# Moving a softmax scale from GpSimd to VectorE, with 1/sum in the PSUM tile of the chunk transposed first, the last output block spread around f tiles 14 and 15, and a rearranged start

## The chip, the cores and the metric

The kernel runs on one core of one Trainium2 chip. The metric is the device time in microseconds (us), lower is better. Every run quoted below is fast unless the text says otherwise; the mean granted TensorE clock was 0.993 to 0.999 of full speed in the profiled runs.

## The reference, cut to what matters

```python
# x (8, 4096, 192), weight_gen (8, 4096, 8 heads, 7 taps)
w = exp(weight_gen - max);  w = w / (sum(w over the 7 taps) + 1e-9)
conv[b, s, h, g] = sum over k of w[b, s, h, k] * x_padded[b, s + k, h, g]     # a causal convolution with its own weights per token
h = conv.reshape(32768, 192) @ w_in        # (192, 2048)
g = h - tanh(h)
out = g @ w_out                            # (2048, 192), float32
```

There are 32 token blocks of 1,024 tokens. For each block a softmax over the taps, seven products (one for each tap), their sum together with a transposition, a first matmul layer with 16 f tiles of 128 columns, `h - tanh(h)`, and a second layer with eight output blocks.

## The kernel before

The work is spread over five engines: ScalarE takes exp, tanh and the copies out of PSUM; VectorE takes the softmax sums, their reciprocals and the subtraction; GpSimd multiplies the softmax (`scale`) and the seven products; TensorE adds the products up in PSUM by multiplying with the identity (the "transposes", three 64-column chunks a block) and does both layers. Blocks are pipelined: while TensorE runs the first layer of block n it also runs the second layer of block n-1, the transposes of block n+1, and GpSimd forms the products of block n+2 with the softmax of n+3 made ready.

These parts are touched. `psum_h` is a pool of three PSUM tiles with one tag, given out in turn to the transposes (`pc`) and to the f tiles of the first layer (`ph`). Whoever asks for a tile gets the one that was used longest ago, and must wait until its last reader is done.

```python
psum_h = tc.tile_pool(name="psum_h", bufs=3, space=PSUM)
...
def softmax_norm(n, bank=None):
    e_t = e_of.pop(n)
    nc.vector.reduce_sum(out=zsum[:], in_=e_t...)
    if bank is None:                                   # every block but the first two
        nc.vector.reciprocal(zr[:], zsum[:])           # 1/sum in SBUF
        wsm_of[n] = (wsm, None, e_t, zr)               # GpSimd will scale: wsm = e_t * zr
        return
    ...
def products(n, ...):
    if e_t is not None:
        first = scale(nc.gpsimd, wsm[:], e_t, zr[:])
    ...                                                # then seven products on GpSimd
def gemm1(n, f):                                       # one f tile of the first layer
    ph = psum_h.tile(..., tag="ph")
    ... 6 matmuls into ph ...                           # "x12" in a timeline is two f tiles
    th = tanh(ph) on ScalarE;  gt = ph - th on VectorE # this subtraction frees ph
...
for n in range(NTOT):
    if n + 3 < NTOT:
        load_wg(n + 3)
        load_x(n + 3)                                  # at the top of the block
    for p in range(J):
        gemm1(n, 2 * p)
        gemm1(n, 2 * p + 1)
        ...
        if 1 <= n < NTOT - 1 and p == 6:               # after f tiles 12 and 13
            sums = conv_sums(n + 1, ((0, 1),), pcs)    # chunks 0 and 1 first
            gemm2((n - 1) * J + 6, between=...)        # mixed with an output block
            conv_out(n + 1, ((0, 1),), pcs)
            conv(n + 1, (2,))                          # then chunk 2
            gemm2((n - 1) * J + 7, 0, FILL)            # 4 matmuls of the last output block
        if p == 6 and n + 3 < NTOT:
            softmax_norm(n + 3)
        if 1 <= n < NTOT - 1 and p == 7:               # after f tiles 14 and 15
            gemm2((n - 1) * J + 7, FILL, NFT)          # its other 28
```

The softmax here doesn't subtract the row's maximum and nothing guards it: scores larger than these inputs give would overflow.

Of the kernel before, what the change touches and what calls it, by code (L numbers as in the profile page):

```python
# [16 lines left out]
def kernel(  # L17
# [8 lines left out]
    nc = tc.nc  # L26
# [52 lines left out]
    last_wsm = {}  # L79
# [19 lines left out]
    def load_x(n):  # L99
# [5 lines left out]
        def rows(p0, p1, r0=0, r1=HALO + J):  # L105
            win = x[b, s0 + p0 * J - HALO + r0 : s0 + p0 * J - HALO + r0 + 1]
            nc.sync.dma_start(  # L107
                out=x_t[p0:p1, r0:r1, :],
                in_=bass.AP(
                    tensor=win.tensor,  # L110
                    offset=win.offset,
                    ap=[[J * D, p1 - p0], [D, r1 - r0], [1, D]],
                ),
            )
# [8 lines left out]
        if n == 0:  # L123
            rows(0, P, HALO, HALO + J)
            rows(16, P, 0, HALO)
            rows(1, 16, 0, HALO)
            no_halo()
        elif s == 0:
            no_halo()
            rows(0, 1, HALO, HALO + J)  # L130
            rows(1, 16)
            rows(16, P)
        else:
            rows(0, P)
        x_of[n] = x_t

    def softmax_exp(n):
        wg_t = wg_of.pop(n)
        e_t = wgpool.tile([P, J, H, K], FP32, name="e_t")
        nc.scalar.activation(  # L140
# [6 lines left out]
    def softmax_norm(n, bank=None):  # L147
# [4 lines left out]
        )  # L152
        wsm = wgpool.tile([P, J, H, K], FP32, name="wsm")
        if bank is None:
            zr = wgpool.tile([P, J * H], FP32, name="zr")
            nc.vector.reciprocal(zr[:], zsum[:])  # L156
            wsm_of[n] = (wsm, None, e_t, zr)
            return

        zr = bank[:, 512 - J * H : 512]  # L160
        nc.vector.reciprocal(zr, zsum[:])
        wsm_v = bank[:, 0 : J * H * K].rearrange("p (j h k) -> p j h k", j=J, h=H)
        scale(nc.vector, wsm_v, e_t, zr)
        last_wsm[0] = scale(nc.vector, wsm[:], e_t, zr)
        wsm_of[n] = (wsm, wsm_v, None, None)
# [8 lines left out]
    def products(n, on_vector=(), order_of=None, sums=None, hooks={}, behind=None):  # L174
        x_t = x_of.pop(n)
        wsm, wsm_v, e_t, zr = wsm_of.pop(n)
        if e_t is not None:
            first = scale(nc.gpsimd, wsm[:], e_t, zr[:])
            if behind is not None:


                order(first, behind, "pace")
# [12 lines left out]
        for k in order_of or range(K):  # L195
            eng, w = (nc.vector, wsm_v) if k in on_vector else (nc.gpsimd, wsm[:])
            eng.tensor_mul(  # L197
                dst[k].rearrange("p c j h g -> p j h c g"),
                x_t[:, k : k + J, :].rearrange("p j (h c g) -> p j h c g", h=H, c=NC),
                w[:, :, :, k : k + 1]  # L200
                .rearrange("p j h (k o) -> p j h k o", o=1)
                .to_broadcast([P, J, H, NC, GC]),
            )
            if k == K - 2 and in_pairs:
# [17 lines left out]
    def conv_sums(n, parts, pcs):  # L222
# [5 lines left out]
        pcs.extend(psum_h.tile([P, 2, HT], FP32, name="pc", tag="ph") for _ in parts)  # L228
        if parts[-1][-1] == NC - 1:
            prods_of.pop(n)  # L230

        for gi in range(max(len(g) for g in prods)):
            for chunks, pc in zip(parts, pcs):
                some = [c for c in chunks if gi < len(prods[c])]
                last = gi == max(len(prods[c]) for c in chunks) - 1
                for c in some:
                    for j in range(JH):
                        col = ((c - chunks[0]) * JH + j) * R
                        for r in range(2):
                            nc.tensor.matmul(  # L240
                                pc[:, r, col : col + R],
# [9 lines left out]
    def conv_out(n, parts, pcs):  # L251
        for chunks, pc in zip(parts, pcs):
            c0, nch = chunks[0], len(chunks)
            nc.scalar.activation(  # L254
                out=conv_of[n][:, c0 : c0 + nch, :].rearrange(
                    "p c (j r t) -> p r (c j) t", r=2, t=R
                ),
                in_=pc[:, :, 0 : nch * JH * R].rearrange("p r (cj t) -> p r cj t", t=R),
                func=ACT.Copy,
            )  # L260
# [28 lines left out]
    LEAD, MIX, FILL = 6, 5, 2  # L289
# [82 lines left out]
    def load_w_in(f0, f1):  # L372

        for c in range(NC):
            src = moe_w_in[c * GC : c * GC + 1, f0:f1]
            dma = nc.gpsimd.dma_start(
                out=w_in[0:R, c, f0:f1],
                in_=bass.AP(
                    tensor=src.tensor,
                    offset=src.offset,  # L380
                    ap=[[G * F, H], [F, GC], [1, f1 - f0]],
                ),
            )
            if f0 == 0:

                order(dma, last_wsm[0], "order of the loads")

    def copy_w_in(f0, f1, eng):
        eng.dma_start(out=w_in[R:P, :, f0:f1], in_=w_in[0:R, :, f0:f1])

    def rest_of_w_in():
        load_w_in(FA, F)

    load_wg(0)
    load_x(0)
    softmax_exp(0)
    softmax_norm(0, obank[0])
    load_wg(1)
    load_x(1)
    load_w_in(0, FA)  # L400
    products(
        0,
        on_vector=(6, 3, 4, 5),
        order_of=(6, 0, 3, 1, 4, 5, 2),
        sums=(6, 3, 0, 4, 5, 1, 2),
        hooks={2: rest_of_w_in},
    )
    softmax_exp(1)
    softmax_norm(1, obank[1])
    load_wg(2)  # L410
    copy_w_in(0, FA, nc.scalar)
    copy_w_in(FA, F, nc.sync)
    products(1, on_vector=(0, 1), hooks={4: load_w_out})
    conv(0, (0, 1), (2,))
    load_x(2)
    for n in range(NTOT):
# [3 lines left out]
        for p in range(J):  # L420
            gemm1(n, 2 * p)
            gemm1(n, 2 * p + 1)
            if n == 0 and p == 1:
                softmax_exp(2)
            if p == 5 and n + 3 < NTOT:
                softmax_exp(n + 3)
            if n >= 1 and (p < 6 or n == NTOT - 1):
                gemm2((n - 1) * J + p)
            if p == 0 and 1 <= n < NTOT - 2:
                products(n + 2, behind=last_sub[0] if n > 1 else None)  # L430
            if n == 0 and p == 7:
                conv(1, (0, 1))
                conv(1, (2,))
# [54 lines left out]
```

## Time and profile before

| | before |
|---|---|
| time, median of 4 runs | 768.37 us |
| a quiet token block, from transposes to transposes | 22.56 us |
| TensorE / GpSimd / VectorE / ScalarE busy in it | 22.56 / 22.18 / 19.93 / 19.77 us |
| second block's first first-layer matmul | 43.05 us |
| one hole of TensorE near 64 us | 3.17 us, and a granted clock of 0.50 for 3.41 us after it |

The block row is the windows view of the kernel before, one quiet block. Its columns are the stretch, its length, then the busy time and number of instructions of TensorE, its weight loads, VectorE, ScalarE and GpSimd, the granted clock, the mean busy share of the DMA engines and GB/s.

```profile
591.44:614.00 22.56, 22.56 (x468) 17.83 (x462) 19.93 (x19) 19.77 (x29) 22.18 (x10) 1.00 0.63 156
```

TensorE is busy for all of it, GpSimd for all but 0.38 us. The other lines of this profile are in the prediction, with what they mean. "issue" in the chain of waits is time in which the engine waits for nothing that the profile shows; `[0.26 <-X]` after an instruction is the idle time before it and what ended it.

### The profile page before, as it was taken

The page shows a single profiled execution, that of the slowest core. Times are in us where ns is not written, and L with a number is a line of the kernel's source. Part 1 is how long each engine was busy: PE and PEld are TensorE (multiplying, and loading weights), DVE is VectorE, ACT ScalarE, POOL GpSimd, SP SyncE. Part 2 cuts the span into 40 slices and gives each one's busy share as a digit, 9 for nine tenths or more (in the row PEclk, how much of TensorE's full clock was granted, in tenths as well). Part 3 has the DMA queues.
Part 4 walks back from the last instruction along what each step waited for, and adds up shares of the span by engine and source line. Part 5 has one row for each costly group of instructions (what it writes and reads, how often), then busy time and mean ns, then how long its engine had stood idle before and what let it go on. Part 6 is the DMA issues. An engine that isn't in the chain of part 4 may idle for free.

```text
span 767.6 us, 32329 instructions
## 1 busy us (share of the span) xinstructions
PE 737.2 (96%) x14784; PEld 577.8 (75%) x14784; DVE 652.8 (85%) x595; ACT 637.1 (83%) x865; POOL 695.3 (91%) x290
## 2 busy tenths in 40 slices
PE   2798999999999999999999999999999999999997
PEld 2276787777777777777777777777778777777777
DVE  7886898888888888889888889888888988888883
ACT  1876888888888888888888888888888888888883
POOL 6999999999999999999999999999999999999100
PEclk9999999999999999999999999999999999999999
DMA  7913776555677555577655567755556765542412
GB/s 216 202 56 87 182 181 161 119 138 150 164 182 176 135 129 145 149 178 183 166 125 129 150 160 182 180 126 139 144 149 175 182 174 114 129 141 77 98 44 84
DMA packets 25989, 111.37 MB, mean 145 GB/s; under 512 B 4815, under 2 KB 9855, under 8 KB 21893
## 3 DMA queue, kind: packets, MB, share of 16 engines
q1 hardware_dynamic: 14830, 77.00, 30.2%
q0 software_dynamic: 10816, 31.99, 25.8%
q8 instruction: 115, 1.88, 1.0%
q10 hardware_dynamic: 208, 0.34, 0.2%
q14 instruction: 20, 0.16, 0.1%
HBM read 54.49 MB, written 25.17 MB: 104 GB/s over the span
## 4 chain that ended last, share of the span: by engine, by line
PE 93%; DVE 3%; POOL 1%; issue 1%; DMA 1%; ACT 0%; SPq 0%; POOLq 0%
PE obank L306 43%; PE ph L273 43%; PE pc L240 6%; DVE gt L285 2%; PE po L341 1%; DMA x_t<-zero 1%; POOL even L197 1%; ACT th L284 0%; POOL odd L197 0%; SPq L107 0%; DVE zr L156 0%; DVE zsum L150 0%; ACT convT L254 0%; SPq L93 0%; DVE out_sb L353 0%
## 5 line engine op out<-in xcount | busy, mean ns | idle before, releaser
L285 DVE TENSOR_TENSOR gt<-ph,th 128x1024 bf16<-128x1024 f32 x512 | 602.7, 1220 | 94.6 <-ACT th L284 92.1
L284 ACT ACTIVATE th<-ph 128x1024 f32<-128x1024 f32 x512 | 497.4, 1022 | 65.9 <-PE ph L273 65.2
L306 PE MATMUL obank<-w_out,gt 64*128 64x192 bf16 x7936 | 399.2, 243 | 1.4 <-issue 0.6
L306 PEld LDWEIGHTS <-gt 64*128 64x128 bf16 x7936 | 351.4, 94 | 52.6 <-issue 1.2
L273 PE MATMUL ph<-convT,w_in 64*128 64x512 bf16 x3072 | 384.8, 378 | 6.3 <-DVE gt L285 5.1
L197 POOL TENSOR_TENSOR even<-x_t,wsm 128x1536 bf16<-128x1536 f32 x94 | 273.0, 2904 | 3.1 <-DMA x_t<-zero 0.7
L197 POOL TENSOR_TENSOR odd<-x_t,wsm 128x1536 bf16<-128x1536 f32 x93 | 270.0, 2904 | 0.0
L273 PEld LDWEIGHTS <-w_in 64*128 64x128 bf16 x3072 | 176.4, 94 | 112.1 <-issue 18.8
L325 ACT ACTIVATE out_sb<-obank 128x192 f32<-128x192 f32 x248 | 82.4, 332 | 30.6 <-PE obank L306 23.5
L197 POOL TENSOR_TENSOR last<-x_t,wsm 128x1536 bf16<-128x1536 f32 x31 | 103.4, 3335 | 0.0
L240 PE MATMUL pc<-ident,even 64*128 64x64 bf16 x2304 | 70.3, 191 | 3.7 <-POOL even L197 2.4
L240 PEld LDWEIGHTS <-even 64*128 64x128 bf16 x2304 | 64.7, 96 | 5.0 <-POOL even L197 2.7
L254 ACT ACTIVATE convT<-pc 128x1024 bf16<-128x1024 f32 x64 | 48.8, 808 | 14.9 <-PE pc L240 14.8
L206 POOL DMA_DIRECT2D even<-odd x29 | 34.9, 1205 | 9.1 <-POOL odd L197 9.1
L168 POOL TENSOR_TENSOR wsm<-e_t,zr 128x448 f32<-128x448 f32 x30 | 41.7, 1391 | 0.0
L240 PE MATMUL pc<-ident,last 64*128 64x64 bf16 x768 | 23.2, 192 | 8.5 <-DVE last L197 8.3
L140 ACT ACTIVATE e_t<-wg_t 128x448 f32<-128x448 f32 x32 | 18.5, 577 | 7.0 <-DMA wg_t<-in_weight_gen_dram 7.0
L240 PEld LDWEIGHTS <-last 64*128 64x128 bf16 x768 | 17.0, 96 | 8.7 <-DVE last L197 8.3
L240 PE MATMUL pc<-ident,odd 64*128 64x64 bf16 x448 | 16.2, 199 | 6.7 <-issue 3.9
L150 DVE TENSOR_REDUCE zsum<-e_t 128x64 f32<-128x448 f32 x32 | 19.5, 609 | 3.0 <-ACT e_t L140 3.0
L156 DVE RECIPROCAL zr<-zsum 128x64 f32<-128x64 f32 x30 | 16.6, 554 | 3.0
L240 PEld LDWEIGHTS <-odd 64*128 64x128 bf16 x448 | 11.8, 100 | 7.4 <-issue 4.2
(20 smaller groups left out, 48.7 us busy)
## 6 DMA issues: line engine op xcount, KB each, us to landing
x_t<-in_x_dram SPq DMA_DIRECT2D x24, 1344.0 KB
even<-odd POOLq DMA_DIRECT2D x29, 1024.0 KB, 8.8
out_dram<-out_sb SPq DMA_DIRECT2D x31, 768.0 KB
x_t<-in_x_dram SPq DMA_DIRECT2D x7, 1176.0 KB
wg_t<-in_weight_gen_dram SPq DMA_DIRECT2D x32, 224.0 KB
x_t<-in_x_dram SPq DMA_DIRECT2D x7, 157.5 KB
x_t<-in_x_dram SPq DMA_DIRECT2D x1, 768.0 KB
w_out<-in_moe_w_out_dram POOLq DMA_DIRECT2D x1, 768.0 KB, 9.1
```

The costliest lines, as they stand in the source:

```text
L140: nc.scalar.activation(out=e_t[:].rearrange("p j h k -> p (j h k)"), in_=wg_t[:].rearrange("p j h k -> p (j h k)"), func=ACT.Exp,)
L150: nc.vector.reduce_sum(out=zsum[:], in_=e_t[:].rearrange("p j h k -> p (j h) k"), axis=AX.X)
L168: return eng.tensor_mul(wsm.rearrange("p j h k -> p (j h) k"), e_t[:].rearrange("p j h k -> p (j h) k"), zr.rearrange("p (n o) -> p n o", ...
L197: eng.tensor_mul(dst[k].rearrange("p c j h g -> p j h c g"), x_t[:, k : k + J, :].rearrange("p j (h c g) -> p j h c g", h=H, c=NC), w[:, : ...
L206: nc.gpsimd.dma_start(out=even[:].rearrange("p i c j h g -> p (i c j h g)")[:, 0:ACC], in_=odd[:].rearrange("p i c j h g -> p (i c j h g)" ...
L240: nc.tensor.matmul(pc[:, r, col : col + R], lhsT=prods[c][gi][r * R : (r + 1) * R, c, 2 * j : 2 * j + 2].rearrange("p j h g -> p (j h g)") ...
L254: nc.scalar.activation(out=conv_of[n][:, c0 : c0 + nch, :].rearrange("p c (j r t) -> p r (c j) t", r=2, t=R), in_=pc[:, :, 0 : nch * JH * ...
L273: nc.tensor.matmul(ph[:, r, :], lhsT=w_in[r * R : (r + 1) * R, c, f * P : (f + 1) * P], rhs=convT[r * R : (r + 1) * R, c, :], start=(c == ...
L284: last_act[0] = nc.scalar.activation(out=th[:], in_=ph_f, func=ACT.Tanh)
L285: last_sub[0] = nc.vector.tensor_sub(gt[:], ph_f, th[:])
L306: mm = nc.tensor.matmul(po[:, 0:D], lhsT=g_of[n][f][r * R : (r + 1) * R, col : col + P], rhs=w_out[r * R : (r + 1) * R, f, :], start=(r == ...
L325: last_act[0] = nc.scalar.activation(out=out_sb[:, j, :], in_=po[:, 0:D], func=ACT.Copy)
```

## The change

The intent: take the scale (1.39 us a block) off GpSimd, the engine that has no free time, and give it to VectorE in a form that was not to disturb GpSimd, with 1/sum in a PSUM tile; let the start overlap better, so that the second block begins earlier. A PSUM tile for 1/sum is at hand just then: that of the chunk transposed first, which ScalarE has just copied out. The chunk order is turned, (2) ahead of (0, 1), and the last output block is spread in three pieces around f tiles 14 and 15.

```diff
 def softmax_norm(n, bank=None, for_gpsimd=True, for_vector=False):
...
+        zr_v = bank[:, 512 - J * H : 512]
+        nc.vector.reciprocal(zr_v, zsum[:])          # 1/sum into the PSUM tile
+        if for_gpsimd:
+            scale(nc.vector, wsm[:], e_t, zr_v)      # VectorE scales
...
 # the end of a block
-                sums = conv_sums(n + 1, ((0, 1),), pcs)
...
+        sums = conv_sums(n + 1, ((2,),), pcs)
+        gemm2((n - 1) * J + 6, between=...)
+        conv_out(n + 1, ((2,),), pcs)
+        conv(n + 1, (0, 1))
+        gemm2((n - 1) * J + 7, 0, FILL)              # FILL = 2:  4 matmuls
+        if n + 3 < NTOT:
+            softmax_norm(n + 3, pcs[0][:, 0])
+        gemm1(n, NFT - 2)                            # f tile 14
+        gemm2((n - 1) * J + 7, FILL, HALF)           # HALF = 9: 14 matmuls
+        gemm1(n, NFT - 1)                            # f tile 15
+        gemm2((n - 1) * J + 7, HALF, NFT)            # 14 matmuls
...
 # the start: x of block 1 held behind block 0's first halo product; w_in's load issued
 # behind the first exp and half of its copy done by ScalarE; the taps of block 0 in pieces on
 # VectorE; softmax of block 2 ahead of the loop, of block 3 in block 1; transposes of
 # block 1 in the gaps of block 0, in the two output banks
+                if p == 3:
+                    sums = conv_sums(1, ((0, 1),), pcs, obank)
+                if 3 <= p <= 6:
+                    some(sums, (3 if p == 3 else 1) * 4 * JH)
```

Three small things go with it: the load of x at the start of a sequence is one transfer instead of three, the order that paces GpSimd by a subtraction of VectorE is put on its first product instead of on its scale, and `LEAD, MIX` (where and how densely transposes are mixed into an output block) are 5, 4 instead of 6, 5.

## The prediction

> **What bounds the kernel now.** I read the busy row and the chain of waits of the page first, then the waits of TensorE, then one undisturbed token block closely, then the start-up.
>
> ```profile
> PE 737.2 (96%) x14784; PEld 577.8 (75%) x14784; DVE 652.8 (85%) x595; ACT 637.1 (83%) x865; POOL 695.3 (91%) x290
> ...
> PE 93%; DVE 3%; POOL 1%; issue 1%; DMA 1%; ACT 0%; SPq 0%; POOLq 0%
> ```
>
> TensorE is busy 96% of the span and carries 93% of the chain that ended last. GpSimd at 91% is close, but its part of the chain is 1%, and in the list of TensorE's waits it occurs only in the start-up (2.4 us in two waits). So relieving GpSimd buys nothing by itself in the middle of the run. The interval from one convT copy to the next is 22.54 to 22.57 us in the quiet blocks; over 28 blocks (91.60 to 727.17) it averages 22.70.
>
> The timeline of one quiet block, TensorE and then VectorE, where the first chunk products are transposed and f tiles 14 and 15 follow:
>
> ```profile
> 610.23 1.48 PE L273 MATMUL ph<-convT,w_in 64*128 64x512 bf16 x12
> ...
> 614.56 1.47 PE L273 MATMUL ph<-convT,w_in 64*128 64x512 bf16 x12
> 615.85 1.34 PE L306 MATMUL obank<-w_out,gt 64*128 64x192 bf16 x28
> 617.01 1.57 PE L273 MATMUL ph<-convT,w_in 64*128 64x512 bf16 x12
> ```
>
> ```profile
> 612.15 2.36 DVE L285 TENSOR_TENSOR gt<-ph,th 128x1024 bf16<-128x1024 f32 x2 [0.26 <-ACT th L284]
> 614.43 0.61 DVE L150 TENSOR_REDUCE zsum<-e_t 128x64 f32<-128x448 f32 x1
> 615.14 0.55 DVE L156 RECIPROCAL zr<-zsum 128x64 f32<-128x64 f32 x1
> 616.48 4.81 DVE L285 TENSOR_TENSOR gt<-ph,th 128x1024 bf16<-128x1024 f32 x4 [0.79 <-ACT th L284]
> ```
>
> The reader is to see that f tile 14 starts at 614.56, while VectorE is still busy with the subtractions of tiles 12 and 13 until 614.5 and then with the sums and their reciprocal until 615.69; after that it has 0.79 us free. In the chain, twelve first-layer matmuls take 1.29 us; the pair at 614.56 takes 1.32 and the one at 617.01 takes 1.39. So the present order costs 0.13 us a block, a small wait for a PSUM buffer that a subtraction frees.
>
> The start-up: VectorE works without a pause through the first block (16 subtractions at 1.13 us, two softmax sums and reciprocals), and the second block's first matmul starts at 43.05. Then there is one real hole:
>
> ```profile
> 63.95 1.02 ACT L254 ACTIVATE convT<-pc 128x1024 bf16<-128x1024 f32 x1 [0.66 <-PE pc L240]
> 68.45 0.60 ACT L254 ACTIVATE convT<-pc 128x512 bf16<-128x512 f32 x1 [3.48 <-PE pc L240]
> ```
>
> ```profile
> 64.29 3.17 issue
> 67.46 0.95 PE pc L240 x29
> 68.41 0.32 PE obank L306 x4
> 68.73 2.44 PE ph L273 x12
> ```
>
> TensorE stands for 3.17 us in the midst of 168 transposes, with nothing recorded that it waits for, and then runs at a granted clock of 0.50 from 68 to 70. With the slow matmuls (2.44 for 1.29, 0.95 for about 0.43, some more) I put the hole at 4.9 us.
>
> [...] the transposes are the densest instruction stretch (15 ns per matmul with its weight load), and the x load of 1.3 MB keeps the DMA share near 1 from 61 to 64. The trace does not name the cause. [...] the scale then reads e_t from SBUF and 1/sum from PSUM. In the start-up that form took 0.62 to 0.63 us beside GpSimd at its usual pace. [...]
>
> **The change part by part, steady blocks.**
>
> Removed: GpSimd's scale, 1.39 us a block, from an engine whose 22.2 us of 22.56 does not set the end: 0. The 0.13 us of buffer wait goes too, because tiles 14 and 15 and the next tile 0 are now 14 second-layer matmuls apart.
>
> Unchanged: the counts of TensorE's work (104 transposes, 96 first-layer and 256 second-layer matmuls a block).
>
> Added: a 0.62 us scale on VectorE, before the subtraction of tile 14. Its 0.79 us of free time nearly holds it, so VectorE's own sequence is hardly pushed. But the PSUM tile of the first-transposed chunk is now released by that scale. There are three such tiles in rotation: tile 12 in X, 13 in Y, the first chunk in Z, the second in X, tile 14 in Y, tile 15 in Z. So tile 15's matmuls wait for the scale.
> - Tile 14 starts at 614.56 as before (the same work lies ahead of it). Six matmuls are 0.65, and 14 second-layer matmuls at 41 ns (1.32/32) are 0.58: tile 15 is ready at 615.79.
> - VectorE: the reciprocal ends at 615.69, 0.04 to the next instruction, 0.62 for the scale: 616.35; with about 0.06 for the signal (as from the subtraction of tile 14 to the matmul it frees at present) TensorE goes on at 616.41. A wait of 0.62 us.
> - From there: 0.65, 0.58 for 14 matmuls, and 1.29 for the next block's tiles 0 and 1: 618.93. Before: 617.01 + 1.39 = 618.40. Net +0.53 a block.
> - Later waits: subtraction 14 would end at 617.5, 15 near 619.3, 0' near 620.6; their buffers are wanted by TensorE at 618.3, 620.3 and 620.9. All in time, so nothing is added and nothing won back.
>
> It occurs in the 28 blocks that still normalise a later one: +14.8. The two others win 0.13 each: -0.3.
>
> **The start-up.** The w_in load is issued at about 4 instead of 6.9, and x of block 1 is held back, so x of block 0 arrives alone (1.8 MB with the weights of the softmax at some 350 GB/s from 2.1: about 7.3 instead of 9.4). GpSimd takes the tap that needs no halo from about 6.2 and then two more at 2.87 us pitch: 14.9 instead of 18.16. With the 1.78 us from there to the first first-layer matmul at present (18.16 to 19.94) that starts at 16.7 instead of 19.94. VectorE: its taps in pieces end near 13.5, the softmax of block 1 near 15.7, two taps of block 1 near 19.1, the softmax of block 2 near 20.3; so its first subtraction starts at 20.3 (before: 22.49), and no softmax lies among the 16 subtractions any more, which end at 38.5 instead of 43.0. The transposes of block 1 go into the two output banks in the gaps that VectorE leaves TensorE. The last tap of block 1 on GpSimd comes at about 33 (before 35.35), early enough. ScalarE's two copies and the third chunk put the second block's first matmul at 38.6 instead of 43.05: -4.5. The softmax of block 3 moves into block 1: 1.15 us on VectorE, of which 0.26 fits in its gap, so about +0.8.
>
> The hole at 64: the same burst of transposes meets the same x load, some 3 to 4 us earlier. But the instruction boundaries, the mix (4 instead of 5) and the load's form shift. I give it one half to vanish: -2.4.
>
> Sum: 768.3 - 4.5 + 0.8 + 14.8 - 0.3 - 2.4 = 776.7, so 776.5.
>
> **The rivals.**
> 1. GpSimd was the hidden bound, and VectorE's scale is hidden. For it: GpSimd has no idle time between blocks, 22.2 busy of 22.56. Against it: the accumulate DMA issued at 618.59 lands in 8.8 us, 7 us and more before its transposes. Then steady blocks gain only the 0.13: 768.3 - 3.7 - 3.9 = about 761, and 756 without the hole.
> 2. The wait is larger: the reciprocal is held by ScalarE's copy, or subtraction 14 is pushed and a second buffer is late. ScalarE's copy of the first chunk should end near 614.4, before the reciprocal, which speaks against it. With 0.3 us more a block: 785.
> 3. The start-up gains less, because the w_in pieces or x of block 1 come late (x of block 1 is only issued after 9.6 and must land by 15.7) or VectorE still has work ahead. Then -1.5 instead of -4.5: 780; with the hole as before, 782.
>
> **Range and chances.** The wait at tile 15 rests on durations that repeat in every block, so I hold it for likely (some 70%): 773 to 782 by the hole and the start-up. Rival 1 has some 20%, and rivals 2 and 3 fill the upper end. Range 762 to 783. Faster by over 2% means below 752.9, which needs everything to go right at once: 0.04. Slower by over 2% means above 783.6: 0.11. Within 2%: 0.85.
>
> **What would show each step.** In the waits of TensorE a new row of first-layer matmuls waiting for VectorE's scale, some 28 times and 0.6 us each; steady blocks of about 23.1 instead of 22.56; GpSimd's busy share down by some 39 us in the whole, with idle time; 1.39 turned into 1.29 at tiles 0 and 1. In the start-up the first subtraction near 20.3 and the second block's first matmul near 38.6. If the blocks stay at 22.4 to 22.6, the wait at tile 15 is wrong, and the time is near 760. The hole is seen as an "issue" piece of over 2 us with a clock of 0.50 after it, or its absence.

Its 350 GB/s are an estimate; in the windows view of before the DMA engines moved 334 GB/s from 2.1 to 9.0 us, at a share of 1.02, which would give 7.5 instead of 7.3. The 0.62 to 0.63 us are the scales at 15.73 and 16.40 in before, beside a product of GpSimd that took 2.90.

## The result, and the profile after

| | before | after |
|---|---|---|
| median of 4 runs | 768.37 us | 781.08 us |
| lowest to highest | 768.07 to 769.78 | 780.94 to 781.58 |
| quiet block | 22.56 us | 23.28 us |
| second block's first first-layer matmul | 43.05 us | 38.31 us |

The ratio of after to before is 1.0163, with a 95% interval of 1.0145 to 1.018: slower, by less than 2%. Ratios here are the mean time of one kernel's fast runs over that of the other's of the same rounds, so they are not quite the ratio of the medians quoted. The predicted 776.5 was 4.6 us low, inside the predicted range.

The busy row and the chain of the page after:

```profile
PE 738.7 (95%) x14784; PEld 576.7 (74%) x14784; DVE 672.4 (86%) x625; ACT 642.0 (82%) x869; POOL 670.1 (86%) x263
...
PE 86%; ACT 4%; issue 4%; DVE 4%; DMA 1%; ACTq 0%; SPq 0%; DVEq 0%
```

GpSimd is relieved (91% to 86%), VectorE hardly more loaded, TensorE does the same matmuls. But TensorE's part of the chain falls from 93% to 86%; ScalarE enters it with 4%, VectorE goes from 3% to 4% and "issue" from 1% to 4%. That is the mark of a wait that has come into every block.

One quiet block after, TensorE in the timeline, from the last second-layer matmuls before f tile 14 on (columns: start, length, engine, line, operation, output and inputs, shapes, number):

```profile
623.74 0.82 PE L290 MATMUL ph<-convT,w_in 64*128 64x512 bf16 x6
624.38 0.76 PE L324 MATMUL obank<-w_out,gt 64*128 64x192 bf16 x14
625.77 0.82 PE L290 MATMUL ph<-convT,w_in 64*128 64x512 bf16 x6 [0.64 <-ACT th L301]
626.42 0.76 PE L324 MATMUL obank<-w_out,gt 64*128 64x192 bf16 x14
627.00 1.48 PE L290 MATMUL ph<-convT,w_in 64*128 64x512 bf16 x12
```

VectorE and ScalarE in the same timeline:

```profile
623.60 0.61 DVE L152 TENSOR_REDUCE zsum<-e_t 128x64 f32<-128x448 f32 x1
624.34 0.56 DVE L162 RECIPROCAL pc<-zsum 128x64 f32<-128x64 f32 x1
625.00 0.62 DVE L175 TENSOR_TENSOR wsm<-e_t,pc 128x448 f32<-128x448 f32 x1
625.72 1.22 DVE L302 TENSOR_TENSOR gt<-ph,th 128x1024 bf16<-128x1024 f32 x1
```

```profile
623.05 1.73 ACT L273 ACTIVATE convT<-pc 128x512 bf16<-128x512 f32 x2
624.67 1.02 ACT L301 ACTIVATE th<-ph 128x1024 f32<-128x1024 f32 x1
```

Tile 15's first matmul (625.77) has 0.64 us of idle time in front of it. Its PSUM tile is the one that holds 1/sum, and VectorE's scale reads it from 625.00 to 625.62. The profile names another releaser, ScalarE's tanh of tile 14 (624.67 + 1.02 = 625.69), which ended a little later. The same in the waits of the kernel after (columns: us in total, times, longest):

```profile
PE ph L290 <- ACT th L301: 15.9, 25, 0.6
...
PE ph L290 <- DVE wsm L175: 0.5, 1, 0.5
```

26 waits of 0.5 to 0.6 us in all, put down to ScalarE but once; in the two other blocks that normalise a later one, blocks 1 and 3 counted from 0, TensorE is late by a hole anyway and tile 15 does not wait. Tile 15 does not use anything that the tanh of tile 14 writes or frees: by the rotation, tile 14 has another PSUM tile. So here a program's own data flow and the profile's inference contradict each other. Which is right is tested below.

Whole blocks, in the windows view of the kernel after (the line to hold against that of before):

```profile
599.77:623.05 23.28, 22.64 (x470) 17.76 (x463) 20.64 (x20) 19.89 (x29) 21.35 (x9) 1.00 0.57 151
```

23.28 = 22.64 busy + 0.64 idle. GpSimd has 1.93 us to spare in the block, as intended, and does nothing with it; in its timeline it stands and waits for the pace that VectorE's subtraction sets:

```profile
608.07 2.90 POOL L201 TENSOR_TENSOR even<-x_t,wsm 128x1536 bf16<-128x1536 f32 x1 [1.64 <-DVE gt L302]
```

The start: the first subtraction on VectorE's timeline, then the second block's first matmul in the chain, then the hole:

```profile
20.46 18.27 DVE L302 TENSOR_TENSOR gt<-ph,th 128x1024 bf16<-128x1024 f32 x16
```

```profile
38.31 1.53 PE ph L290 x12
...
59.56 2.61 issue
62.17 0.59 PE pc L249 x29
```

All 16 subtractions of the first block now run without a softmax among them, and the second block starts 4.74 us earlier. The hole has moved with the burst of transposes, from 64.29 to 59.56, and has not gone.

**Where the time went, as a ledger** of the two profiled runs (spans 767.6 and 779.8, so +12.2), cut at the first transposes of the fourth block and of the last block, both read from the timelines of TensorE:

| stretch | before | after | difference |
|---|---|---|---|
| up to the fourth block's first transposes | 89.72 | 84.36 | -5.36 |
| from there to the last block's first transposes, 28 blocks | 635.55 | 652.59 | +17.04 |
| from there to the end | 42.33 | 42.85 | +0.52 |

In the middle row, 27 blocks (the first of the 28 waits falls into the row above) at 23.28 instead of 22.56 and one (the last, without a softmax) at 22.63 would make +19.5. It is only 17.0 because the blocks of before are not all quiet: their surplus over 22.56 adds up to 3.9 us (blocks of 22.97, 22.88, 23.17, 23.27 among them), while after has 1.4 over 23.28, all but 0.1 in its first two. In before TensorE has small "issue" pauses of 0.15 to 0.56 us in eight of these blocks, 2.2 us together; in after the wait at tile 15 stands at 0.64 us in nearly every block, and from the third of these blocks on there is no other pause of note. One thing differs that can account for it. GpSimd's scales in the timeline of before:

```profile
576.94 1.42 POOL L168 TENSOR_TENSOR wsm<-e_t,zr 128x448 f32<-128x448 f32 x1
599.59 1.41 POOL L168 TENSOR_TENSOR wsm<-e_t,zr 128x448 f32<-128x448 f32 x1
622.23 1.42 POOL L168 TENSOR_TENSOR wsm<-e_t,zr 128x448 f32<-128x448 f32 x1
```

One round of GpSimd takes 22.65 us: more than its 22.18 us busy, by the gaps between its instructions, and more than the 22.56 of a quiet TensorE block. So in before GpSimd runs freely and its round drifts against TensorE's, and with it the moment at which an x buffer comes free and the next load of x begins. In after it waits for the pace in each block, and the loads keep one place. I had read the busy time as if it were the round.

### The profile page after: what moved, and what is told of

It is laid out like the page before. It is cut to its first block, busy times and chain, and to the rows that moved or that the text cites. A ratio compares the mean times of both kernels' runs of the same rounds, so it can differ in the third digit from the quotient of the medians.

```text
span 779.8 us, 32319 instructions
## 1 busy us (share of the span) xinstructions
PE 738.7 (95%) x14784; PEld 576.7 (74%) x14784; DVE 672.4 (86%) x625; ACT 642.0 (82%) x869; POOL 670.1 (86%) x263
## 3 DMA queue, kind: packets, MB, share of 16 engines
q8 instruction: 115, 1.88, 1.0%
## 4 chain that ended last, share of the span: by engine, by line
PE 86%; ACT 4%; issue 4%; DVE 4%; DMA 1%; ACTq 0%; SPq 0%; DVEq 0%
PE ph L290 40%; PE obank L324 39%; PE pc L249 6%; ACT th L301 4%; DVE gt L302 2%; DMA x_t<-in_x_dram 1%; PE po L359 1%; DVE odd L201 0%; DVE even L201 0%; DVE zsum L152 0%; ACT out_sb L343 0%; DVE wsm L175 0%; ACT convT L267 0%; ACT convT L273 0%; DVE pc L162 0%
## 5 line engine op out<-in xcount | busy, mean ns | idle before, releaser
L302 DVE TENSOR_TENSOR gt<-ph,th 128x1024 bf16<-128x1024 f32 x512 | 604.9, 1219 | 83.8 <-ACT th L301 81.3
L324 PEld LDWEIGHTS <-gt 64*128 64x128 bf16 x7936 | 355.5, 94 | 58.4 <-ACT th L301 0.8
L201 POOL TENSOR_TENSOR even<-x_t,wsm 128x1536 bf16<-128x1536 f32 x93 | 273.8, 2944 | 39.7 <-DVE gt L302 39.5
L201 POOL TENSOR_TENSOR odd<-x_t,wsm 128x1536 bf16<-128x1536 f32 x93 | 273.8, 2944 | 0.0
L249 PE MATMUL pc<-ident,even 64*128 64x64 bf16 x2256 | 58.7, 191 | 0.9 <-issue 0.6
L273 ACT ACTIVATE convT<-pc 128x512 bf16<-128x512 f32 (+1 forms) x63 | 50.6, 804 | 10.5 <-PE pc L249 7.4
L249 PEld LDWEIGHTS <-even 64*128 64x128 bf16 x2304 | 56.4, 96 | 1.7 <-issue 1.0
L249 PEld LDWEIGHTS <-last 64*128 64x128 bf16 x768 | 20.8, 96 | 9.8 <-POOL last L201 9.6
L152 DVE TENSOR_REDUCE zsum<-e_t 128x64 f32<-128x448 f32 x32 | 19.5, 609 | 3.0 <-ACT e_t L141 3.0
L175 DVE TENSOR_TENSOR wsm<-e_t,pc 128x448 f32<-128x448 f32 x28 | 17.4, 621 | 2.9
L249 PEld LDWEIGHTS <-odd 64*128 64x128 bf16 x448 | 15.5, 100 | 4.6 <-issue 2.7
L162 DVE RECIPROCAL pc<-zsum 128x64 f32<-128x64 f32 x28 | 15.7, 561 | 3.7
```

The lines of the kernel that those rows point to most:

```text
L152: nc.vector.reduce_sum(out=zsum[:], in_=e_t[:].rearrange("p j h k -> p (j h) k"), axis=AX.X)
L175: return eng.tensor_mul(wsm.rearrange("p j h k -> p (j h) k"), e_t[:].rearrange("p j h k -> p (j h) k"), zr.rearrange("p (n o) -> p n o", ...
L201: mul = eng.tensor_mul(dst[k][:, :, j0:j1].rearrange("p c j h g -> p j h c g"), x_t[:, k + j0 : k + j1, :].rearrange("p j (h c g) -> p j h ...
L249: nc.tensor.matmul(pc[r][:, col : col + R] if home else pc[:, r, col : col + R], lhsT=prods[c][gi][r * R : (r + 1) * R, c, 2 * j : 2 * j + ...
L273: nc.scalar.activation(out=out, in_=pc[:, :, 0:cols].rearrange("p r (cj t) -> p r cj t", t=R), func=ACT.Copy,)
L302: last_sub[0] = nc.vector.tensor_sub(gt[:], ph_f, th[:])
```

## The experiments

**The theories.** A: tile 15 waits for VectorE's scale, through the rotation of the three PSUM tiles. B: the longer block comes from the new order itself (ScalarE's two copies, its tanh as the wait row says, the spread output block), whoever scales. For the hole a third, H: a burst of transposes that meets the load of x for a later block makes TensorE stand; a burst without a load beside it does not. (The expectations of e6 and e9 word it as instruction fetch that comes late, which was a conjecture then; what the traces show of it stands under what stands behind the holes.) Times of "before" are 768.45, 769.05 and 768.75 us (e1 to e4; e5 to e8; e9 to e12). All kernels gave correct results.

### e1: the scale back on GpSimd, everything else as after

```diff
-            softmax_norm(n + 3, pcs[0][:, 0])
+            softmax_norm(n + 3)
```

> The changed kernel, but in the steady blocks the 1/sum goes to SBUF again and GpSimd scales; the start-up, the order of the chunks and the spreading of the f tiles stay. Theory A (tile 15 waits until VectorE's scale releases the PSUM tile): the 0.6 us idle of TensorE before tile 15 disappears, blocks fall from 23.28 to about 22.6 us (not to 22.43, because the two last blocks of the changed kernel, which have no scale, took 22.63), and the time to about 762 us. Theory B (tile 15 waits for the tanh of tile 14, which the profile names as releaser): tanh 14 ends at the same place, the wait stays, 781 us. Theory C (GpSimd was the hidden bound): GpSimd gets its 1.4 us a block back and becomes the bound; over 765 us, with TensorE waits on GpSimd.

Measured: 769.28 us, ratio to before 1.001 (0.9995 to 1.0025). TensorE's timeline of the block that answers to those above:

```profile
614.83 0.82 PE L290 MATMUL ph<-convT,w_in 64*128 64x512 bf16 x6
...
616.11 0.88 PE L290 MATMUL ph<-convT,w_in 64*128 64x512 bf16 x6
...
617.35 1.57 PE L290 MATMUL ph<-convT,w_in 64*128 64x512 bf16 x12
```

No wait in front of tile 15: it starts 1.28 us after tile 14, where after took 2.03. Quiet blocks are 22.64 us, and ScalarE's copies, its tanh and the order are those of after. So the wait is the scale's: A holds and B falls, the wait row of after named the wrong engine. The total missed its expectation by 7 us, though. With the scale back on GpSimd the pauses are back too (blocks of 23.19, 23.52, 23.49, 24.35), and "issue" pieces of 2.60, 1.62, 1.33 and 1.54 us stand in the chain (at 59.05, 88.13, 110.08, 340.92). Of the 5.9 us won up to the fourth block's transposes, 2.2 are lost because the quiet block is 22.64 and not 22.56 (28 times 0.08), and 4.0 because the pauses are larger than in before. That made the holes a question of their own.

### e2: the scale done twice

```diff
             scale(nc.vector, wsm[:], e_t, zr_v)
+            if twice:
+                scale(nc.vector, wsm[:], e_t, zr_v)
```

> The changed kernel with VectorE's scale of the steady blocks done twice, one after the other into the same tile (result unchanged). Theory A: the release comes one scale later, about 0.65 us a block, so the wait before tile 15 grows from 0.64 to about 1.3 us, blocks to 23.9, the time to about 799 us (781.1 + 28 x 0.65). Theory B: the tanh of tile 14 does not move, the wait stays at 0.64 us and the time at 781 to 784.

Measured: 799.05 us, ratio 1.04 (1.0384 to 1.0415); quiet blocks 23.93 us, 0.65 more than after: one more scale, one to one on the path. The waits of this kernel:

```profile
PE ph L292 <- DVE wsm L177: 34.1, 27, 1.3
```

With the second scale ending well after the tanh, the profile names the right releaser too, 27 times, in 27 of the 28 such blocks. A is shown from both sides.

### e3: tile 15 only after the whole output block

```diff
-        gemm2((n - 1) * J + 7, FILL, HALF)
+        gemm2((n - 1) * J + 7, FILL, NFT)
         gemm1(n, NFT - 1)
-        gemm2((n - 1) * J + 7, HALF, NFT)
```

All 28 second-layer matmuls now lie between tiles 14 and 15, 0.57 us more, nearly the wait.

> The changed kernel with all 28 second-layer matmuls of the last output block ahead of tile 15 instead of 14. Under theory A the release falls at the same moment and TensorE has 0.58 us more work ahead of it: the wait before tile 15 shrinks from 0.64 to about 0.06 us (0.81 to 0.23 from start to start), blocks from 23.28 to about 22.7, the time to about 765 us. Theory B expects the same here; this run tells whether the wait can be covered by order alone, or whether tile 15, and the next tiles 0 and 1 in a row, bring a new wait on a subtraction (then over 770 us).

Measured: 778.2 us, ratio 1.013 (1.0113 to 1.0147), quiet blocks 23.12. Nearly all of the wait is back, elsewhere. VectorE and TensorE in the timeline, then the waits:

```profile
624.40 5.75 DVE L302 TENSOR_TENSOR gt<-ph,th 128x1024 bf16<-128x1024 f32 x5 [0.74 <-ACT th L301]
```

```profile
626.82 0.82 PE L290 MATMUL ph<-convT,w_in 64*128 64x512 bf16 x6 [0.22 <-DVE gt L302]
```

```profile
PE ph L290 <- DVE gt L302: 9.2, 35, 1.0
```

Tile 15 and the next block's tiles 0 and 1 now run in one row with nothing between them. Tile 15 still comes about 0.25 us late (622.49, with the matmuls before it ending near 622.24), and the three tiles ask for freed buffers faster than VectorE subtracts (1.13 us apart, five in a row), so a later tile waits for a subtraction. The spreading of the output block is what the rotation needs; the wait cannot be hidden by shifting the filler alone.

### e4: 1/sum in the tile of the second transposes

```diff
-        sums = conv_sums(n + 1, ((2,),), pcs)
+        sums = conv_sums(n + 1, ((0, 1),), pcs)          # chunk order of before
...
-            softmax_norm(n + 3, pcs[0][:, 0])
+            softmax_norm(n + 3, pcs2[0][:, 0])           # pcs2: chunk 2, transposed second
```

`LEAD, MIX` go back to 6, 5 with the chunk order, here and in e5, e8 and e9.

That tile is taken next by the following block's tile 0, one step later than tile 15.

> The changed kernel with the two chunk tiles in the order of before (the full tile first, the half-full one second), and 1/sum in the half-full, now second, tile. By the rotation of the three PSUM tiles the next tile 0 and not tile 15 waits for the scale. Theory A: no wait before tile 15 (0.81 us saved); but the reciprocal waits for ScalarE's second copy, so the scale ends some 0.5 us later, tile 0 waits 0.1 or less, and subtraction 14 is pushed by some 0.4 us, for which tile 1 waits about 0.4 us: blocks of 22.8 to 23.0, about 770 us. Theory B: the wait before tile 15 stays, about 781 us.

Measured: 770.52 us, ratio 1.0025 (1.001 to 1.004); blocks of 22.82 us, from the sixth on all equal to 0.01 (GpSimd is relieved here too). The scale has not become free, but of 0.72 us a block against before 0.26 are left. The run changes the chunk order too, but by e1 the order of after costs only 0.08 us without the scale. So the cost is in the main a matter of which of the rotating tiles holds 1/sum. This is the cheap repair of the change: 10.6 us below the 781.08 of after. They were run at other times.

### e5: the start of after, the blocks of before

```diff
-        sums = conv_sums(n + 1, ((2,),), pcs)
+        sums = conv_sums(n + 1, ((0, 1),), pcs)
...
-            softmax_norm(n + 3, pcs[0][:, 0])
+            softmax_norm(n + 3)
         gemm1(n, NFT - 2)
-        gemm2((n - 1) * J + 7, FILL, HALF)
         gemm1(n, NFT - 1)
-        gemm2((n - 1) * J + 7, HALF, NFT)
+        gemm2((n - 1) * J + 7, FILL, NFT)
```

Of the small things of the change, the pace order on the first product and the single load of x stay as in after.

> The start-up of the changed kernel with the steady blocks of before (full chunk tile first, GpSimd scales, tiles 14 and 15 side by side). It measures the start-up alone. The second block's first matmul at 38.3 instead of 43.05 us, nothing else changed: 768.4 - 4.7 = 763.7 us if the hole near 60 us costs as much as the one of before at 64 us (4.9 us), 762.5 if it costs the 3.75 us of the changed kernel, 759 if it is absent. By subtraction the steady part of the change then costs 781.1 minus this, 17 to 19 us.

Measured: 768.93 us, ratio 1.0003 (0.9988 to 1.0018). The expectation failed: nothing left of a start that is worth over 4 us. The transposes of the fourth block begin at 82.83 instead of 89.72, but the blocks from there on have 10.0 us of surplus over 22.56, before had 3.9: of the 6.9 us won, 6.1 are given back in the middle. The chain shows where, with the two largest pieces behind that point (others of 2.62 and 1.91 stand at 59.45 and 341.04):

```profile
87.23 2.28 issue
...
109.58 2.34 issue
```

The second of these in the windows view, in three single microseconds (columns as above):

```profile
109.00:110.00 1.00, 0.58 (x29) 0.46 (x23) 1.00 (x2) 0.33 (x1) 1.00 (x2) 1.00 1.03 422
110.00:111.00 1.00, 0.00 (x0) 0.00 (x0) 0.90 (x3) 0.00 (x0) 1.00 (x1) 1.00 0.88 343
113.00:114.00 1.00, 1.00 (x10) 0.52 (x6) 0.00 (x0) 0.73 (x2) 1.00 (x1) 0.50 0.06 16
```

TensorE stops in the midst of the transposes while the DMA engines are as good as fully busy (343 to 422 GB/s; a load of x, 1,344 KB, has just ended, at 109.29, and the 768 KB of an output block are under way), and afterwards the clock is at 0.50. This fits H: the start that is earlier by 4 to 7 us moves later bursts of transposes onto later loads of x.

### e6 and e8: only the load of x for block 4 moved away

```diff
-            load_x(n + 3)
+            if n != 1:
+                load_x(n + 3)
...
         gemm1(n, NFT - 2)
+        if n == 1:
+            load_x(4, last_sub[0])        # behind the subtraction of f tile 14
```

e6 does this to after, e8 to e5.

> The changed kernel with one edit: the load of x for block 4 is held until the subtraction of tile 14 in block 1, so that it does not lie beside the 168 transposes near 58 us. If the hole of 2.6 us in the middle of those transposes comes from instruction fetch behind that load: the hole is gone, the clock stays at 1.00, the time falls by about 3.7 to 777.4 us, provided that the load lands in time for GpSimd (it needs it near 75 us). If the load is not the cause: the hole stays at 2 to 3 us and the time at 781.

> The start-up of the changed kernel, the steady blocks of before and the late load of x for block 4: the candidate that should beat both kernels. If the load causes the hole: 763 - 3.7 to 4.9, about 759 us. If not: the same as the run with the old blocks alone, about 763.

Measured: e6 782.85 us, ratio 1.0181 (1.0166 to 1.0196), 5.5 us over what was expected; e8 768.63 us, ratio 1.0 (0.9983 to 1.0017), 9.6 us over. Both totals were missed. The chain of e6:

```profile
61.27 0.67 issue
...
88.39 2.10 issue
```

The hole near 60 shrank from 2.61 to 0.67, as H says; but the next one, 0.95 us at 89.32 in after, grew to 2.10, beside an output block and a part of a load of x. The transposes before it also waited 1.26 us, until 84.09, for the accumulating DMA of GpSimd's products, which landed at 83.95. In e8 likewise: the hole near 60 shrank to 0.69, and pieces of 2.67 and 1.31 stand at 86.08 and 110.49. The hole is not a thing of one place, and one load moved out of its way only moves it on.

### e9, e12 and e10: every load of x for block 4 and later behind the burst

```diff
-            load_x(n + 3)
+            if n < 1:
+                load_x(n + 3)
...
+        if n + 3 < NTOT:
+            load_x(n + 3, last_sub[0])    # issued behind the subtraction of f tile 13
```

e9 does this to e5, e12 to after; e10 does it to before, with `load_x` given an order behind that subtraction.

> The start-up of the changed kernel with the steady blocks of before, and in every block from the second on the load of x for the block three ahead is held until the subtraction of f tile 13, that is to the end of the burst of transposes. Theory H (the holes are instruction fetch that comes late when a burst of transposes lies inside an x load): no more holes of over 1 us after the second block, blocks of 22.56 us throughout, and the 4.7 us that the start-up wins are kept and the holes' 9 us of before won as well: 755 to 758 us. Rival H2 (the holes come from anything else, for instance from TensorE being too far ahead of GpSimd): the holes stay and the time is about 768 us, or more if the late loads hold GpSimd up.

> The changed kernel with the x loads held as in the run with all x late. Blocks stay at 23.28 us by theory A, since the wait before tile 15 has nothing to do with the loads; the holes near 60 and 88 us go by theory H: 781.1 - 4 to 5 = 776 to 777.5 us. Its distance to the run with old blocks and all x late is then the clean cost of the steady part: 28 x 0.72 = 20 us.

> The kernel before with that one edit alone (x loads held to the end of the burst from the second block on). Theory H: the hole of 3.17 us at 64 us and its half clock go, 768.5 - 4.9 = about 763.5 us, a little less if the small pieces of 0.15 to 0.5 us go too. H2: 768.5 us.

| | before | e10 (before, x late) | e9 (e5, x late) | e12 (after, x late) |
|---|---|---|---|---|
| median, us | 768.75 | 763.06 | 761.37 | 776.93 |
| ratio to before (95%) | | 0.9925 (0.9911 to 0.994) | 0.9903 (0.9888 to 0.9918) | 1.011 (1.0094 to 1.0125) |
| fourth block's first transposes | 89.72 | 84.93 | 81.3 | 80.98 |
| surplus of the 28 blocks after it, over | 3.9 (22.56) | 2.1 (22.56) | 4.4 (22.56) | -0.6 (23.28) |

(The column of before takes its last two rows from its own profile above. In the last column the block without a softmax counts with 22.64, as in the ledger; the surplus is below nought because the transposes at 80.98 are themselves 0.67 us late, behind the accumulating DMA, and the block after them takes 22.66.) The hole of before, in e10's chain, and the stretch before it in the windows view, once of e10 and once of before:

```profile
63.53 0.70 issue
```

```profile
60.00:63.80 3.80, 3.53 (x173) 3.44 (x170) 3.44 (x5) 2.47 (x4) 3.80 (x2) 1.00 0.02 4
```

```profile
60.00:64.30 4.30, 4.29 (x181) 4.00 (x177) 4.02 (x5) 2.97 (x6) 4.30 (x3) 1.00 0.89 249
```

The same transposes at a DMA share of 0.02 instead of 0.89 leave a pause of 0.70 us instead of 3.17, and no half clock after it. e10 met its expectation within 0.5 us: 5.7 us for moving one line. H holds for the large hole; the 0.70 us that is left has no load beside it.

e9 beats both kernels and is the best of all, but stays 3 to 6 us above its expectation. Its big holes have gone; the surplus has another cause now. The engines' part of its chain, and a row of its waits:

```profile
PE 49%; POOL 42%; DMA 4%; issue 2%; ACT 1%; DVE 1%; POOLq 0%
```

```profile
PE pc L249 <- DMA even<-odd: 1.6, 3, 0.6
```

GpSimd carries 42% of the chain. Its round is 22.64 us here as well, and its products of the early blocks come only about 2 us sooner than in before (the scale of block 3 starts at 54.19 instead of 56.42). So TensorE, at 22.56, catches up with it, and then the transposes wait for the accumulating DMA behind its products; the chain of waits runs through GpSimd's start for the same reason. After the first of these waits TensorE stands for 2.1 us more behind that DMA: 1.13 at 150.56 (the profile puts it down to VectorE, but the DMA landed at 150.43), 0.53 and 0.44. 28 blocks at 0.08 more would be 2.2, of 4.4 us of surplus; "issue" pauses of 0.56 and 0.42 are another part. With the large holes gone, the engine that the change relieved has become a limit. e12's total met its expectation: 23.28 in every block from the second of these on, but for the last, without a softmax. It has the relief, but the wait at tile 15 costs it more than that. Its distance to e9, expected as 20 us, is 15.6: e9 is not at 22.56 throughout.

### e11: before, with the load of x put into the burst

```diff
         for p in range(J):
             gemm1(n, 2 * p)
+            if n >= 1 and n + 3 < NTOT and p == 4:
+                load_x(n + 3, last_sub[0])
```

The loads at the top of the block fall away as in e10.

> The kernel before with the x loads from the second block on held to a moment some 2 us ahead of the f tile 12, so that each load of about 10 us lies across the burst of its block (the dose in the other direction; GpSimd still gets x in time by some 5 us). Theory H: holes of 1 to 3 us in most blocks, the time well over 790 us, up to 850. H2: no new holes, about 768 us.

Measured: 793.47 us, ratio 1.0329 (1.0312 to 1.0346). That is the "well over 790" of its expectation only just. Its chain:

```profile
63.66 3.85 issue
...
348.27 3.88 issue
```

Other pieces of 1.46 to 2.67 us stand at 183.72, 230.58, 257.25, 513.17 and 631.63, and in all about 12 of the 28 blocks are clearly longer (up to 28.17). So the load in the burst makes holes, and more of them than anything else that I changed: H again. But holes in most blocks were expected, and fewer than half have one, though the loads were moved alike in all. H does not name all of what is needed; what is missing is found below, under what stands behind the holes.

### e7: 1/sum in SBUF instead of PSUM

```diff
-            softmax_norm(n + 3, pcs[0][:, 0])
+            softmax_norm(n + 3, in_sbuf=True)     # reciprocal to zr, scale on VectorE from zr
```

> The changed kernel with VectorE scaling as now, but from a 1/sum in SBUF, so that no PSUM tile is held. Theory A: no wait before tile 15. What it tells besides is why 1/sum was put into PSUM: if two SBUF inputs contend with GpSimd, the scale takes over 0.62 us (up to 2 or 3) or GpSimd's instruction beside it grows by some 0.6 us; subtraction 14 is pushed by the same and tile 1 of the next block waits for it. Blocks of 22.6 (no contention, about 762 us) to 23.3 us (781 us). If contention is absent, the PSUM detour was not needed.

Measured: two runs in the fast state, 778.56 and 774.26 us, and two in the slow one, 789.53 and 793.92; the ratio of the fast ones is 1.0099 (1.0065 to 1.0133). The scale in VectorE's timeline, in the first blocks and in a late one:

```profile
88.13 7.45 DVE L177 TENSOR_TENSOR wsm<-e_t,zr 128x448 f32<-128x448 f32 x1
118.96 3.61 DVE L177 TENSOR_TENSOR wsm<-e_t,zr 128x448 f32<-128x448 f32 x1
145.95 3.38 DVE L177 TENSOR_TENSOR wsm<-e_t,zr 128x448 f32<-128x448 f32 x1
...
624.27 0.68 DVE L177 TENSOR_TENSOR wsm<-e_t,zr 128x448 f32<-128x448 f32 x1
```

With both inputs in SBUF the same scale takes up to 7.45 us beside a busy GpSimd. The first three blocks were 30.82, 26.99 and 25.10 us long; after that the kernel settled with the scale in a moment in which GpSimd stood, and blocks of 22.64. In after the four scales that start at 60.32 to 136.03 lie wholly beside a product of GpSimd and take 0.62 us all the same: that one input in PSUM keeps the scale short there, 0.62 us against 3.38 to 7.45, is shown. From the fifth on, the scale of after too begins in about the last 0.27 us of a product and runs into GpSimd's pause. That the kernel as a whole needs the PSUM tile is not shown: the two fast runs of e7 are 2.5 and 6.8 us below the 781.08 of after. They were run at other times. That the late blocks are better than those of after is a gift of timing; with runs that differ by 20 us I would not build on it.

## Why the prediction was right, and where it was off

By its own steps:

- **The wait of tile 15 for VectorE's scale.** Right in cause (e1, e2), in place and nearly in number (26 of the 28 blocks that normalise a later one). Mis-sized: tile 15 was to start 1.85 us after tile 14 (616.41 less 614.56), and starts 2.03 after it. Two terms were too small. The scale ends 1.88 us after the start of tile 14 (625.62 less 623.74), not 1.79, in the main because 0.10 us lie between reciprocal and scale instead of 0.04. And 0.15 us pass from the end of the scale to tile 15's matmul, not 0.06. The blocks are therefore 23.28 instead of 23.09. I had taken the signal from a matmul whose weights were loaded ahead. Here the weight load comes after the release too, in the timeline of weight loads:

```profile
625.74 0.36 PEld L290 LDWEIGHTS <-w_in 64*128 64x128 bf16 x6 [0.83 <-issue]
```

  In the records of the trace a wait for VectorE stands in front of tile 15's weight load, and one for ScalarE at the matmul behind it. That explains the 0.09 us and also why the profile put the matmul's wait down to ScalarE; but it is read from the trace, no run took it apart.
- **The 0.13 us of spreading.** Right in the blocks with the wait: the next block's tile 1 follows 2.61 us after its tile 0 (627.00 to 629.61), no delay. Wrong in the last block and in e1, where there is no wait: 22.63 and 22.64 instead of about 22.43. In e1 VectorE stands 0.86 us until the tanh of tile 14 is done, which begins behind ScalarE's two copies (1.73 us instead of 1.51 in before); so its subtractions are no earlier than before, and tile 1 follows tile 0 only after 2.71 us (617.35 to 620.06). In after this touches one block, some 0.2 us.
- **GpSimd's relief is worth nothing in the middle.** Nearly right, and argued wrongly. Its scales fell from 41.7 to 2.9 us as predicted, and it stood for 39.5 us behind the pace. But it was no engine with time to spare: its round of 22.65 us was longer than TensorE's quiet block and shorter only than the average one (22.70). The relief is worth what lies between 22.56 and 22.70, at most some 4 us, of which the ledger shows 2.5; that the steadier loads are the way in which it comes is inferred. Rival 1, with its 761, was wrong because the wait is real, and right in that GpSimd was the next limit (e9).
- **The start-up.** Right: 20.46 for the first subtraction (predicted 20.3), 38.31 for the second block (38.6).
- **Softmax of block 3 in block 1: +0.8.** It cost about 0.07. That block's TensorE has slack, since only half of the second layer's matmuls run in its first output block; from its tile 0 to its tile 13 pass 17.02 us in before and 17.09 in after.
- **The hole, an even chance to vanish.** It stayed, 2.61 instead of 3.17 us. What stands behind it is below. The first row of the ledger, -5.36, is made of -4.74 for the start, +0.07 for the softmax and some -0.7 for the rest (the hole, its half clock, the end of block 1), where the steps had -4.5, +0.8 and -2.4 + 0.53. The sums, -5.36 and -5.6, agree by luck: the softmax that cost next to nothing paid for the hole that stayed.
- **The sum.** The ledger's middle row holds 27 blocks with the wait and one without; the prediction had 27 x 0.53 - 0.13 = +14.2 for them, the ledger has +17.04: the wait and the last block make it 5.3 larger, the small pauses that are gone 2.5 smaller. These last were in no step: the sum took the average block (22.70, with its pauses) as the base and added a wait to it, as if the pauses would stay. The end has 0.52 us that I have not traced. In all +12.2 against +8.4; without errors in both directions it would have been further off.

Rival 2 (a larger wait, 785) came nearest of the rivals in its cause: the wait was larger, but by 0.19 us a block and not 0.3. The number of rival 3, 780 to 782, fits 781.08 best, by luck: its cause did not occur in the start itself. Its form came true in e5: there the gain of the start was lost to holes later.

**What stands behind the holes.** No run was made for this, but the kept traces show what goes with them. A queue of the kind "instruction" moves 115 DMA packets of 16,384 bytes in a run (116 in e12), one for about every 256 instructions of TensorE. Counted over the records of all 14 traces from 40 us on, TensorE has 65 "issue" pauses of over 0.1 us. Every one of them stands at the same count of TensorE's instructions (matmuls, weight loads and the few others that are recorded), 193 to 195 beyond a multiple of 256, and ends 1.23 to 1.60 us after the end of such a packet. At the 1,492 other places with that count the packet had ended in time, 0.93 us or more before TensorE came there. Four of the pauses:

| us | before | e10 | after | e5 |
|---|---|---|---|---|
| TensorE passes such a place | 61.92 | 61.16 | 57.24 | 104.81 |
| the next packet moves | 65.07 to 66.15 | 61.59 to 62.76 | 59.72 to 60.64 | 109.52 to 110.48 |
| TensorE stands at the next such place | 64.29 to 67.46 | 63.53 to 64.24 | 59.56 to 62.17 | 109.58 to 111.92 |

In before and e10 TensorE needs 2.37 us from one of these places to the next within the burst. The packet itself takes about 1 us, and 1.3 to 1.5 us more pass until TensorE goes on, so even e10's early packet leaves a pause; in before it moves only 3.15 us after the place was passed, when the DMA share has fallen from 0.87 (64 to 65) to 0.12 (65 to 66). So H is a special case: a hole comes where a packet is late between two places that TensorE passes quickly. This also tells why e11 has no hole in many blocks.

**What stays open.** What decides how late a packet is: outside the bursts, packets 3 to 5 us late are common in these traces (about a third of them in before and in after) and cost nothing there. That other loads hold it up is shown for the hole of before by e10; in general it is inferred, since no run moved the queue or the places. Not tried either: e4 with all loads of x late, which by its blocks of 22.82 and with relief for GpSimd should leave fewer holes.

## What to carry to other kernels

Before a value is put into a spare buffer of a rotation, ask who gets that buffer next: the instruction that reads the value becomes part of the path of the next owner, and one place further on in the rotation the same scale cost 0.26 us a block instead of 0.72. When a change at the start shifts everything that follows, look for new coincidences of bursts and loads before believing the gain; here moving the loads out of the bursts (5.7 us for one line) was the only single edit that made the kernel before faster. When pauses without a visible cause recur, count the instructions between them: here an equal count modulo 256 (193 to 195 at all 65 pauses) led to the packets. An engine's round, from one block's instruction to the next block's same one, says whether it has time to spare; its busy time does not. And where the profile's releaser is no one who touches the buffer, trust the data flow and test it by lengthening the suspect, as e2 does.

## What these traces show of the hardware

- At 1,492 of the places counted above the packet of the instruction queue had come in time, at 65 not: in dense streams of short instructions beside large loads TensorE stood for 2.61 us in after, 3.17 in before and up to 3.88 in e11, and moving the loads (e10) brought 3.17 down to 0.70.
- A clock of 0.50 followed the 3.17 us of before and the 2.61 us of after, for 3.41 us each time, and pauses of 2.34 us (e5, at 109.58) and 2.10 us (e6, at 88.39); none followed one of 2.28 us (e5, at 87.23).
- Where the wait for a buffer sits on the weight load, as at tile 15 in after, the trace shows the load 0.12 us after the release (625.74 after 625.62) and the matmul at 0.15 us (625.77), against about 0.06 where the load was done ahead (before, the matmul that the subtraction of tile 14 frees).
- With one SBUF input the scale took 0.62 us in every block of after; with two, 7.45, 3.61 and 3.38 us in the first blocks of e7. In all three cases the scale ended only 0.48 to 0.49 us after a product of GpSimd that was followed by a pause of GpSimd, and the scale of 7.45 us lay across the starts of two products (88.92, 91.78).
